# Weight sums moved from VectorE to GpSimd, and all tasks ordered anew, in a threshold attention and gated feed-forward kernel

## The chip, the cores and the metric

The kernel runs on one core of a Trainium2 chip. A core has five engines, each with its own instruction queue that is worked off strictly in order: TensorE (PE, matmuls; its weight loads are shown as PEld), VectorE (DVE), ScalarE (ACT), GpSimd (POOL) and SyncE (SP, which here only issues transfers). Data lies in SBUF, 128 partitions wide; matmuls write to PSUM banks. The metric is the device time of one execution in microseconds; lower is better.

## What is computed

Everything is float32. Attention comes first: batch 8, 8 heads, 576 tokens, head width 64. In each row of scores only the values within `tau` = 0.02 of the row's maximum are kept; a softmax over them weights the values. Its output, laid out as 4608 tokens by 512, goes through a feed-forward layer of width 2048.

```
scores = q @ k^T / 8;  scores = where(scores >= rowmax - tau, scores, -1e9)
attn   = exp(scores - rowmax);  attn = attn / (sum(attn) + 1e-9);  x = attn @ v      # (8,8,576,64) -> (4608,512)
h = x @ w_in;   g = h * sigmoid(1.702 h);   out = g @ w_out
```

## The kernel before

**Attention** works on 32 pairs of heads, numbered n; four pairs make one batch of 576 tokens. For a pair, PE writes scores transposed into PSUM (`scores`, L590), ACT copies them to SBUF (`keep`, L607), DVE reduces them to a row maximum (`in_groups`, L613, and the small steps after it), DVE subtracts the maximum (`sub`, L687), ACT masks and exponentiates (`mask` L694, `exps` L698), and PE multiplies by the values (`values`, L709). Pairs 0 to 3 have their softmax sums made by PE too. `place_x` (DVE, L813) divides by the sums and writes a slice of x into one of six `xT` tiles. From pair 6 on, the `values` of one pair and the `scores_run` of a later one run on PE as one uninterrupted stretch.

**Feed-forward** works on 18 blocks of 256 tokens, in order; one chain of dependencies (`ffn`) strings all its PE work together. Blocks 0 and 1 run the first layer plainly (`mm1_0`, L886, then `tanh` L843 on ACT and `gelu_0` L892 on DVE). The other products are done in Strassen-like form: seven products of quarter matrices (P1, P2, P6, P7, P4, P5, P3) instead of eight, where the quarters of weights and of tokens are first added or subtracted. `product1` (L954) does this for the first layer of one block, `product4` (L1127) for two blocks at once from block 7 to block 12, `product` (L1431) for the second layer. The last 1024 tokens, blocks 14 to 17 (`TAIL`), use the form twice over: each of the seven products is again split into seven (`product2` L1278, `product3` L1387). For that second level the sums of quarters of quarters of the weights are needed: three 128x512 sums for each of seven matrices of each layer, 42 in all.

**These 42 sums** are made by `scrap_sum` (L1197) long before they are used, one instruction per sum, and written to DRAM by SP. Eight of the fourteen triples are made along with blocks 3 to 6 (`EARLY_EXTRAS`, in the function `seven`): the triple's tile is an `xT` tile, and two transfers (`extra_out`, L1201) carry it out. The other six are made along with block pairs 7, 9 and 11 (`LATE_EXTRAS`, in `seven4`), two triples each: every sum goes to the one buffer `scrap`, and the next may begin only when the transfer of the last (`scrap_out`, L1207) is done. In the tail `extra_in` (L1240) and `extra2_in` (L1315) bring them back.

**Weights of the first layer's sums** for `product4` flow back from DRAM through four small buffers: `w_flow` (L1104), a transfer issued from POOL's queue, twelve per pair of blocks. A block pair's first two go out when the previous blocks no longer use the buffers' space, and P6 is the first product that reads them.

**Weight conversion.** The inputs `moe_w_in` and `moe_w_out` come as 64-bit floats and are turned into float32 in 32 pieces of 128x512: SP loads a piece into a staging area (`load_w`, L510), ACT computes one part in two steps (`cv_power` L520, `cv_power2` L524), DVE the other and joins them (`cv_whole` L538, `cv_end` L545). Pieces 0 to 15 are `w_in`, 16 to 31 `w_out`. A staging slot comes free when `cv_end` is done.

**The order.** Each engine's program order is not written by hand. Every step is a `task` with an engine, a planned cost, a rank, what it must follow and which buffers it takes and gives back. `run_in_order` plays all tasks through in planned time: an engine that is free takes, of the tasks that are ready, the one with the lowest rank, and the instructions are emitted in that order. Ranks are the pair's number plus a bias for each function; the tables `EARLY`, `SECOND`, `LATER`, `CV`, `W_RANK` and `L_RANK` hold the biases. Attention on PE goes ahead of feed-forward whenever it is ready. 40 short matmul tasks (`stay_warm`, L1497) are taken only where nothing else is ready in the plan.

Of the kernel before, what the change touches and what calls it, by code (L numbers as in the profile page):

```python
# [32 lines left out]
def kernel(  # L33
# [96 lines left out]
    for x in ("raw0", "raw1", "qkT0", "qkT1", "mb"):  # L130
# [3 lines left out]


    EARLY = {
        "add_row": 15.24,
        "cross_max": 16.53,
        "exps": 169.66,
        "in_groups": 24.3,  # L140
        "keep": 18.51,
        "load_qk": 52.9,
        "load_v": 77.19,
        "mask": 220.69,
        "one_row": 73.01,
        "over_halves": -24.07,
        "over_tiles": 93.0,
        "place_x": 110.06,
        "row_in": 2.01,
        "row_out": -23.95,  # L150
        "scores_run": 0.25,
        "spread_max": -9.31,
        "spread_sums": 55.95,
        "sub": 109.63,
        "sums_by_pe": 219.69,
        "turn_in": 106.44,
        "turn_rows": -16.16,
        "turned": 157.69,
        "values": 15.27,
    }  # L160
    SECOND = {
        "add_row": 48.97,
        "cross_max": -30.15,
        "cross_sums": 46.61,
        "exps": 425.25,
        "in_groups": 788.95,
        "keep": 52.62,
        "load_qk": -8.72,
        "load_v": 50.95,
        "mask": 273.1,  # L170
        "over_halves": 13.47,
        "over_tiles": 10.11,
        "place_x": -14.67,
        "prep": 130.42,
        "row_in": -47.42,
        "row_out": 60.46,
        "scores_run": -14.82,
        "spread_max": -16.4,
        "sub": 29.57,
        "sums_in": 53.13,  # L180
        "sums_out": -17.8,
        "turn_rows": -30.52,
        "turn_sums": 63.82,
        "values": -7.11,
    }
    LATER = {
        "add2": -163.47,
        "add3": -23.7,
        "copy2": 51.25,
        "copy3": 34.37,  # L190
        "cross_max": 60.81,
        "cross_sums": 61.03,
        "exps": 93.29,
        "in_groups": 10.85,
        "keep": 85.17,
        "load_qk": -13.0,
        "load_v": -2.27,
        "mask": 11.12,
        "over_halves": -26.94,
        "over_tiles": -36.69,  # L200
        "place_x": -13.68,
        "prep": 24.88,
        "s_level1": -6.85,
        "s_level2": -6.85,
        "scores_run": 22.76,
        "silu2": 83.51,
        "spread_max": -74.31,
        "sub": -0.09,
        "sums_in": -524.28,
        "sums_out": -75.26,  # L210
        "turn_sums": 83.71,
        "values": -57.82,
    }
    CV = {
        "cv_end": 69.28,
        "cv_power": -47.14,
        "cv_power2": -20.47,
        "cv_whole": -4.05,
        "load_w": 14.98,
    }  # L220

    LAG = {"PE": 0.26, "DVE": 0.18, "ACT": 0.22, "POOL": 0.18, "SP": 0.1}
# [957 lines left out]
    def scrap_sum(second, x, k):  # L1180
        u1 = u2 = scrap
        if x in SOONER[second]:
            if k == 0:
                places["extra", second, x] = x_home()
            u1, u2 = (places["extra", second, x][:, ts(z, BANK)] for z in range(2))
        if second:
            y = right2(x)
            b11, b12, b21, b22 = (y[:, ts(c, 4), ts(n, HT)] for c in range(2) for n in range(2))
            u1, u2 = four(u1), four(u2)
            o, a, b, op = ((u1, b12, b11), (u2, b22, u1), (u1, b21, u2))[k] + (ALU.subtract,)  # L1190
        else:
            y = left1(x)
            a11, a12, a21, a22 = (y[:, c, ts(f, BANK)] for f in range(2) for c in range(2))
            o, a, b, op = (
                (u1, a21, a22, ALU.add), (u2, u1, a11, ALU.subtract), (u1, a12, u2, ALU.subtract)
            )[k]
        nc.vector.tensor_tensor(out=o, in0=a, in1=b, op=op)  # L1197

    def extra_out(second, x, part):
        n, m = ((2, 0), (1, 2))[part]  # L1200
# [329 lines left out]
    FFU = 1.727  # L1530
    T_RANK = FIRST

    W_RANK = (51.17, 144.32, 134.71, 686.68, 50.64, 279.44)
    W_TIME = 1.8
    WARM = 40
    ROUND_BY_ACT = range(0)
# [415 lines left out]
    def seven(blk):  # L1952
        b = -(-(blk + 1) * BLK // S) - 1
        xs = [placed[n] for n in range(NPAIR * (b + 1))]
        xd = []
        if not w_done:
            w_sums()
        a = None
        for second_layer, n in EARLY_EXTRAS.get(blk, ()):
            for k in range(3):  # L1960
                a = task(
                    "DVE", 0.6, FIRST, scrap_sum, second_layer, n, k,
                    after=[w_done[-1], t_ready[-1], ffn[-1], a], take=("xT",) if k == 0 else (),
                )
                if k:
                    a = task("SP", 0.55, FIRST, extra_out, second_layer, n, k - 1, after=[a], take=RING[0])
                    a = transfer("DMS", (3.0, 1.5)[k - 1], a, 2, give=RING[0] + (("xT",) if k == 2 else ()))
            (extra_out_done, extra2_out_done)[second_layer][n] = a
        for x in range(4):
            xd.append(task("DVE", 0.34, FIRST, x_sum, blk, x, after=(xd[-1:] or xs) + last1))  # L1970
        keeps, adds, gs = {}, {}, {}

        def gelued(y, f, h, after):
            gs.setdefault((f, h), {})[y] = task(
                "ACT", 0.5, FIRST, silu1, y, f, h, after=after,
                give=("psM",) if (f, h) == (1, 0) else (),
            )

        for x in (P1, P2, P6, P5, P7, P4, P3):
            for y in range(2):  # L1980
                after = ffn[-1:] + xs
                if x in (P6, P7, P4, P5):
                    after = after + xd[{P6: 1, P7: 2, P4: 3, P5: 0}[x]:][:1]
                if x in (P6, P7, P5, P3):
                    after = after + [w_done[{P6: 1, P7: 2, P5: 0, P3: 3}[x]]]
                if x in (P6, P7, P4):
                    after = after + [keeps[{P6: P1, P7: P6, P4: P7}[x], y]]
                if x == P3:
                    after = after + [adds[P5, 0], adds[P5, 1]]
                ffn.append(task(  # L1990
                    "PE", 1.785, LAST, product1, blk, x, y, after=after,
                    take=("psM",) if x == P1 else ("psA",) if x in (P2, P5) and y == 0 else (),
                    give=("xT",) if x == P3 and y else (),
                ))
                if x in (P1, P6, P7):
                    keeps[x, y] = task("ACT", 0.5, FIRST, keep1, x, y, after=ffn[-1:])
                if x in (P2, P3) and y:
                    for z in range(2):
                        adds[x, z] = task(
                            "DVE", 0.6, FIRST, add1, x, z,  # L2000
                            after=ffn[-1:] + [keeps[{P2: P1, P3: P6}[x], z]],
                            give=("psA",) if z else (),
                        )
                        if x == P3:
                            gelued(z, 0, 1, [adds[P3, z], gs[1, 1][1]])
                if x == P7:
                    adds[P5, y] = task(
                        "DVE", 0.6, FIRST, add1, P5, y, after=[keeps[P7, y], ffn[-2 - y]],
                    )
                if x == P4:  # L2010
                    gelued(y, 1, 0, ffn[-1:])
                    if y:
                        for f, h, z in ((0, 0, P2), (1, 1, P5)):
                            for w in range(2):
                                gelued(w, f, h, [adds[z, w], gs[1, 0][w]])
        last1[:] = ffn[-1:]
        sums = [
            task("DVE", 1.33, FIRST, s_sums, blk, y, after=[gs[x][y] for x in ((0, 0), (0, 1), (1, 1))])
            for y in range(2)
        ]  # L2020
        minus = [task("DVE", 0.6, FIRST, s_minus, blk, y, after=[sums[y]]) for y in range(2)]
        second(blk, {P1: gs[0, 0], P2: gs[1, 0], P4: gs[1, 1]}, sums, minus)
# [8 lines left out]
    def seven4(blk):  # L2031
# [11 lines left out]
        a = None  # L2043
        for second_layer, x in LATE_EXTRAS[blk]:
            for k in range(3):
                a = task("DVE", 0.6, FIRST, scrap_sum, second_layer, x, k, after=freed + [t_ready[-1], a])
                a = task("SP", 0.55, FIRST, scrap_out, second_layer, x, k, after=[a], take=RING[0])
                a = transfer("DMS", 1.4, a, 2, give=RING[0])
            (extra_out_done, extra2_out_done)[second_layer][x] = a
# [270 lines left out]
            next_blk += 1  # L2320

    crossed = {"max": [], "sums": []}
    L_RANK = (6.9, -26.88, 69.44, 31.9, 9.2, 38.16, 10.43, 63.15, 25.98, 364.83, 169.13, -0.14, 11.11, -6.6, 5.42, 34.59, 27.46, 64.99, 61.43, -2.14, 71.89, -4.67, 27.56, 35.73)

    def load_rank(n, which):
        return L_RANK[3 * n + which] if 3 * n < len(L_RANK) else 0.0
# [242 lines left out]
```

## Time and profile before

| | |
|---|---|
| median of 3 runs | 1224.37 us (1223.91 to 1226.27) |
| profiled execution, span from first to last instruction | 1224.7 us |
| PE / PEld busy | 1206.5 us (99%) / 995.8 us (81%) |
| DVE busy | 1077.1 us (88%), 1683 instructions |
| ACT busy | 797.6 us (65%), 1197 instructions |
| POOL busy | 69.3 us (6%), 114 instructions |
| DMA, mean over the span | 111 GB/s, 136.09 MB |

How to read it: the profiled execution is listed with its span alone, which lies 0.3 us above the median of the runs. A row of a group gives the instruction's line, its engine, what it writes and reads, its shape, how often it ran, its total busy time and the mean of one, and how long the engine stood idle just before it. A row of a timeline gives start, duration and the same names, and in brackets the idle time ahead of it with what ended that. PE's busy time counts matmuls whose ends are modelled, so that neighbours overlap by a fraction of a microsecond. Trace counts of float32 matmuls are twice the number in the program's listing.

### The profile page before, as it was taken

To read this page: it belongs to the slowest core of one execution; us is meant where nothing else is said; L and a number is where in the kernel's file an instruction comes from. 1 tells how busy PE (TensorE), PEld (TensorE's weight loads), DVE (VectorE), ACT (ScalarE), POOL (GpSimd) and SP (SyncE) were. 2 spreads that over 40 slices of the span, in tenths; PEclk is the share of its full clock that TensorE was granted. 3 is DMA by queue.
4 is the path that set the end of the run, shared out by engine and by line. 5 is a ranking of instruction groups with operands and counts; after the bars stand their busy time and mean duration, and the time that the engine had idled before them with its cause. 6 is when DMAs were issued, how large, how long until landed. Compare 5 with 4: busy or idle time off the path is not lost.

```text
span 1224.7 us, 26240 instructions
## 1 busy us (share of the span) xinstructions
PE 1206.5 (99%) x10672; PEld 995.8 (81%) x10672; DVE 1077.1 (88%) x1683; ACT 797.6 (65%) x1197; POOL 69.3 (6%) x114
## 2 busy tenths in 40 slices
PE   8999999999999999999999999999999999999998
PEld 5656777797978888888777777787787797999998
DVE  6989998878898998898699977998799989999797
ACT  6999977675765766684686468756875676340340
POOL 0111231100000000000100010001100000000000
PEclk9999999999999999999999999999999999999999
DMA  8957769492323241224423252225322351444443
GB/s 222 249 108 190 173 142 170 103 210 65 93 50 110 49 120 48 75 72 135 101 67 99 66 133 72 59 77 128 92 49 67 87 139 39 139 129 140 140 137 104
DMA packets 201193, 136.09 MB, mean 111 GB/s; under 512 B 146864, under 2 KB 163376, under 8 KB 200944
## 3 DMA queue, kind: packets, MB, share of 16 engines
q1 hardware_dynamic: 189712, 110.21, 34.0%
q0 software_dynamic: 10672, 23.90, 9.4%
q8 instruction: 84, 1.38, 0.5%
q10 hardware_dynamic: 688, 0.30, 0.1%
q14 instruction: 37, 0.30, 0.1%
HBM read 103.28 MB, written 23.75 MB: 104 GB/s over the span
## 4 chain that ended last, share of the span: by engine, by line
PE 88%; ACT 8%; DMA 2%; DVE 1%; issue 1%; SPq 0%; DVEq 0%; ACTq 0%
PE ops L1431 28%; PE pv L709 10%; PE ps L590 10%; PE hps L954 7%; PE hps L1127 7%; PE ps L954 5%; PE ps L1127 5%; PE hps L1278 4%; PE ops L1387 4%; PE ps L1278 3%; PE ps L1387 3%; ACT arena L698 2%; ACT arena L694 2%; PE hps L886 2%; ACT arena L607 2%; DMA arena<-in_moe_w_in_dram 1%
## 5 line engine op out<-in xcount | busy, mean ns | idle before, releaser
L613 DVE TRANSPOSE_TENSOR_REDUCE part<-arena 128x36 f32<-128x1152 f32 x300 | 363.8, 1239 | 52.6 <-ACT arena L607 40.2
L607 ACT COPY arena<-ps 128x576 f32<-128x576 f32 x288 | 171.2, 642 | 95.6 <-PE ps L590 95.5
L694 ACT ACTIVATE arena<-arena 128x1152 f32<-128x1152 f32 (+1 forms) x160 | 164.6, 1064 | 66.6 <-DVE arena L687 66.2
L1431 PE MATMUL ops<-w_out,arena 128*128 128x256 f32 x896 | 203.0, 381 | 0.1
L1431 PEld LDWEIGHTS ops<-w_out,arena 128*128 128x128 f32 x896 | 168.5, 190 | 28.5 <-issue 5.3
L687 DVE TENSOR_TENSOR arena<-arena 128x1152 f32<-128x1152 f32 (+1 forms) x150 | 180.9, 1241 | 0.7
L698 ACT ACTIVATE arena<-arena,shift 128x1152 f32<-128x1152 f32 (+1 forms) x160 | 179.7, 1156 | 1.4
L590 PE MATMUL ps<-arena 64*64 64x288 f32 x2304 | 172.1, 408 | 8.0 <-ACT arena L607 6.1
L709 PE MATMUL pv<-arena 64*64 64x288 f32 x2176 | 159.2, 405 | 0.0
L590 PEld LDWEIGHTS ps<-arena 64*64 64x64 f32 x2304 | 81.9, 132 | 71.5 <-ACT arena L607 29.7
L1431 PE MATMUL ops<-arena 128*128 128x256 f32 x576 | 129.1, 379 | 0.0
L709 PEld LDWEIGHTS pv<-arena 64*64 64x64 f32 x2176 | 80.3, 133 | 53.0 <-issue 9.0
L1431 PEld LDWEIGHTS ops<-arena 128*128 128x128 f32 x576 | 109.2, 190 | 15.8 <-issue 0.9
L1292 ACT COPY arena<-hps 128x512 f32<-128x512 f32 x44 | 25.7, 584 | 59.5 <-PE hps L1278 59.5
L632 ACT ACTIVATE other<-red,minus_gap 32x18 f32<-32x18 f32 x118 | 36.2, 307 | 35.1 <-DVE red L622 33.6
L1104 POOL DMA_DIRECT2D arena<-wrow x36 | 19.5, 540 | 619.0 <-DVE arena L1197 321.8
L886 PE MATMUL hps<-xT,w_in 128*128 128x256 f32 x232 | 51.2, 381 | 0.9 <-DVE arena L892 0.9
L886 PEld LDWEIGHTS hps<-xT,w_in 128*128 128x128 f32 x232 | 43.6, 190 | 8.6 <-DVE arena L892 1.5
L1453 DVE SCALAR_TENSOR_TENSOR osb<-ops,osb 128x256 f32<-128x256 f32 x98 | 39.2, 411 | 11.5 <-PE ops L1431 10.5
L954 PEld LDWEIGHTS hps<-xT,w_in 128*128 128x128 f32 x384 | 44.2, 192 | 1.5 <-issue 0.9
L954 PE MATMUL hps<-xT,w_in 128*128 128x128 f32 x384 | 45.3, 276 | 0.0
L1127 PE MATMUL hps<-xT,w_in 128*128 128x256 f32 x192 | 43.4, 379 | 0.0
(228 smaller groups left out, 1859.9 us busy)
## 6 DMA issues: line engine op xcount, KB each, us to landing
arena<-in_v_dram SPq DMA_DIRECT2D x128, 144.0 KB
arena<-exu SPq DMA_DIRECT2D x42, 256.0 KB
arena<-ext SPq DMA_DIRECT2D x39, 256.0 KB
arena<-wrow POOLq DMA_DIRECT2D x36, 256.0 KB, 3.3
arena<-in_k_dram SPq DMA_DIRECT2D x112, 72.0 KB
arena<-in_q_dram SPq DMA_DIRECT2D x112, 72.0 KB
out_dram<-osb SPq DMA_DIRECT2D x28, 256.0 KB
arena<-row_s SPq DMA_DIRECT2D x48, 144.0 KB
```

What stands on the lines that cost most here:

```text
L590: nc.tensor.matmul(ps[ts(c, KT), h, 0:SH], lhsT=mats[n, 1][ts(h, D), ts(j, KT)], rhs=mats[n, 0][ts(h, D), ts(c, SH)], start=True, stop=True,)
L607: nc.scalar.copy(out=sT[n, t][:, u], in_=pss.pop((n, j))[:, :, 0:SH])
L613: nc.vector.tensor_reduce(out=stats[n, op][:, t * 2 * QB : min(2 * t + 2, NK) * QB], in_=sT[n, t].rearrange("p u h (g d) -> p (u h g) d", ...
L687: engine.tensor_tensor(out=s, in0=s, in1=mbs[n].unsqueeze(1).to_broadcast(list(s.shape)), op=ALU.add if n in BY_DMA else ALU.subtract,)
L694: nc.scalar.activation(out=s, in_=s, func=AF.Prelu, alpha=STEEP)
L698: nc.scalar.activation(out=s, in_=s, func=AF.Exp, scale=SCALE, bias=shift)
L709: nc.tensor.matmul(o[c][ts(h, D), 0:SH], lhsT=left(j, h)[ts(c, KT)], rhs=sT[n, t][ts(c, KT), u, h, :], start=(j == 0), stop=(j == NK - 1),)
L886: nc.tensor.matmul(hidden[j][:, ts(i, BLK)], lhsT=w_in[:, c, ts(j, P)], rhs=xTs[i][:, c, :], start=(c == 0), stop=(c == NDC - 1), skip_gro ...
L954: nc.tensor.matmul(o[:, ts(j, HT)], lhsT=left[:, c, ts(4 * y + j, P)], rhs=right[:, c, :], start=(x in (P1, P2, P5) and j + c == 0), stop= ...
L1127: nc.tensor.matmul(o[:, ts(j, BLK)], lhsT=left[:, c, ts(j, P)], rhs=right[:, c, :], start=(x in (P1, P2, P5) and j + c == 0), stop=(j + c ...
L1278: nc.tensor.matmul(o[:, ts(j, HT)], lhsT=left[:, ts(j, P)], rhs=right, start=(m in (P1, P2, P5) and j == 0), stop=(j == 3), skip_group_che ...
L1431: nc.tensor.matmul(banks[blk][k][:, ts(o, HM)], lhsT=left[:, j, :], rhs=right[:, j, :], start=(j == 0), stop=(j == HF - 1),)
```

## The change

`scrap_sum` issues its instruction on GpSimd, and the two places that make its tasks book it on POOL with a planned cost of 1.3 us, where it was DVE with 0.6 us. All six tables of ranks have new values. Nothing else differs: the same instructions, transfers, buffers and dependencies; on which engine 42 of them stand, and the order on every engine, are new.

```diff
@@ scrap_sum
-        nc.vector.tensor_tensor(out=o, in0=a, in1=b, op=op)
+        nc.gpsimd.tensor_tensor(out=o, in0=a, in1=b, op=op)
@@ seven: EARLY_EXTRAS
-                    "DVE", 0.6, FIRST, scrap_sum, second_layer, n, k,
+                    "POOL", 1.3, FIRST, scrap_sum, second_layer, n, k,
@@ seven4: LATE_EXTRAS
-                a = task("DVE", 0.6, FIRST, scrap_sum, second_layer, x, k, after=freed + [t_ready[-1], a])
+                a = task("POOL", 1.3, FIRST, scrap_sum, second_layer, x, k, after=freed + [t_ready[-1], a])
@@ tables of ranks, all entries; some of them
     EARLY = {
...
-        "exps": 169.66,
+        "exps": 218.659396,
...
     LATER = {
-        "add2": -163.47,
+        "add2": 218.879808,
...
-    W_RANK = (51.17, 144.32, 134.71, 686.68, 50.64, 279.44)
+    W_RANK = (48.948553, 218.656324, 220.911367, 648.238789, 209.699298, 477.491922)
...
-    L_RANK = (6.9, -26.88, 69.44, 31.9, 9.2, 38.16, 10.43, ...
+    L_RANK = (-88.352359, -377.791989, 203.787298, 98.253766, 49.342752, -419.169055, -251.720956, ...
```

More of the change, by code (lines that the diff above doesn't have):

```diff
@@ L136 @@
     EARLY = {
-        "add_row": 15.24,
-        "cross_max": 16.53,
-        "exps": 169.66,
[L140 to L159, printed above, removed]
+        "add_row": -26.779956,
+        "cross_max": -186.11076,
+        "exps": 218.659396,
+        "in_groups": -921.329572,
+        "keep": -376.476703,
+        "load_qk": 28.45392,
+        "load_v": 55.937037,
+        "mask": 258.382077,
+        "one_row": 754.390311,
+        "over_halves": -177.607232,
+        "over_tiles": -242.559764,
+        "place_x": 353.472828,
@@ L160 @@
+        "row_in": -524.546255,
+        "row_out": -204.477791,
+        "scores_run": 73.864427,
+        "spread_max": -665.338509,
+        "spread_sums": -255.466111,
+        "sub": 276.088418,
+        "sums_by_pe": 395.294969,
+        "turn_in": 1536.802593,
+        "turn_rows": -980.064642,
+        "turned": 86.363115,
+        "values": -93.163536,
     }
     SECOND = {
[L162 to L184, printed above, removed]
+        "add_row": 276.088418,
@@ new lines @@
+        "cross_max": -240.949838,
+        "cross_sums": -329.737322,
+        "exps": 504.025884,
+        "in_groups": 987.755038,
+        "keep": 46.111798,
+        "load_qk": -533.474947,
+        "load_v": 332.525097,
+        "mask": 481.823863,
+        "over_halves": -194.246828,
+        "over_tiles": 543.631566,
+        "place_x": 800.597733,
+        "prep": 454.948868,
+        "row_in": -31.868144,
+        "row_out": 80.112526,
+        "scores_run": -23.727141,
+        "spread_max": 634.529675,
@@ L185 @@
+        "sub": 806.709122,
+        "sums_in": 528.330009,
+        "sums_out": 403.59979,
+        "turn_rows": -550.558759,
+        "turn_sums": -21.685664,
+        "values": 818.914814,
     }
     LATER = {
-        "add2": -163.47,
[L188 to L212, printed above, removed]
+        "add2": 218.879808,
+        "add3": -4.036609,
+        "copy2": -530.184332,
@@ new lines @@
+        "copy3": 209.512485,
+        "cross_max": 1588.737584,
+        "cross_sums": 546.442989,
+        "exps": 614.129479,
+        "in_groups": 183.39928,
+        "keep": 353.976442,
+        "load_qk": 354.397262,
+        "load_v": 796.965227,
+        "mask": 4.965175,
+        "over_halves": 55.173625,
+        "over_tiles": 792.89621,
+        "place_x": -14.016573,
+        "prep": 1023.214781,
+        "s_level1": 1308.273433,
+        "s_level2": 381.073959,
+        "scores_run": -30.208042,
@@ L213 @@
+        "silu2": 49.468221,
+        "spread_max": 417.352117,
+        "sub": 46.78672,
+        "sums_in": -951.376181,
+        "sums_out": 718.483673,
+        "turn_sums": 144.651892,
+        "values": -771.795118,
     }
     CV = {
[L215 to L219, printed above, removed]
+        "cv_end": 5.647379,
+        "cv_power": -62.099737,
+        "cv_power2": -63.051811,
+        "cv_whole": 224.118761,
@@ L220 @@
+        "load_w": 41.452962,
     }
@@ L2322 @@
     crossed = {"max": [], "sums": []}
-    L_RANK = (6.9, -26.88, 69.44, 31.9, 9.2, 38.16, 10.43, 63.15, 25.98, 364.83, 169.13, -0.14, 11.11, -6.6, 5.42, 34.59, 27.46, 64.99, 61.43, -2.14, 71.89, -4.67, 27.56, 35.73)
+    L_RANK = (-88.352359, -377.791989, 203.787298, 98.253766, 49.342752, -419.169055, -251.720956, 316.979634, 531.734811, 464.681494, 298.790272, -81.491014, 99.216053, 450.74533, 707.475464, 354.348049, -186.433338, -612.234764, 270.826085, -446.603159, 423.489084, 582.149219, 643.218533, -435.166825)
     def load_rank(n, which):
```

## The prediction

> **What bounds the kernel now.** I read the page first (busy times, clock, chain), then stretches of time, then the engines' timelines where PE is not full.
>
> ```profile
> span 1224.7 us, 26240 instructions
> ...
> PE 1206.5 (99%) x10672; PEld 995.8 (81%) x10672; DVE 1077.1 (88%) x1683; ACT 797.6 (65%) x1197; POOL 69.3 (6%) x114
> ...
> PE 88%; ACT 8%; DMA 2%; DVE 1%; issue 1%; SPq 0%; DVEq 0%; ACTq 0%
> ```
>
> The chain that ended last is PE for 88% of the span, ACT for 8%. Where the 8% lies, the next view tells: it gives, for a stretch, its length and the busy time of PE, PEld, DVE, ACT, POOL, then granted clock, DMA share, GB/s.
>
> ```profile
> 0.00:150.00 150.00, 135.29 (x1667) 90.96 (x1668) 128.68 (x202) 137.24 (x202) 27.79 (x51) 0.99 0.76 187
> 150.00:1200.00 1050.00, 1049.70 (x8816) 883.55 (x8815) 931.03 (x1435) 659.48 (x993) 41.52 (x63) 1.00 0.40 101
> 1200.00:1225.00 25.00, 21.50 (x193) 21.31 (x191) 17.41 (x48) 0.83 (x3) 0.00 (x0) 1.00 0.31 96
> ```
>
> From 150 to 1200 us PE stands idle for 0.30 us in all, at full clock. DVE, which the change relieves, has 931 of 1050 us there and PE never waits for it long enough to show. So the time is: when PE's unbroken stretch begins, plus a fixed amount of PE work, plus the end. Only the first 150 us and new stalls can move it.
>
> The head, on PE:
>
> ```profile
> 108.39 1.99 PE L886 MATMUL hps<-xT,w_in 128*128 128x256 f32 x8
> 111.27 26.17 PE L886 MATMUL hps<-xT,w_in 128*128 128x256 f32 x120 [0.89 <-DVE arena L892]
> ...
> 146.21 1.25 PE L590 MATMUL ps<-arena 64*64 64x288 f32 x16 [1.52 <-ACT arena L607]
> ...
> 176.00 1.44 PE L1497 MATMUL up<-eye,ones 64*64 64x128 f32 x12
> 177.51 7.17 PE L1431 MATMUL ops<-w_out,arena 128*128 128x256 f32 x32
> ```
>
> Feed-forward starts at 108.39, waits 0.89 us for the first `gelu_0`, then runs; 1.52 us are lost at 146 behind ACT's `keep`; at 176 PE fills 1.44 us with warm-up matmuls. And on ACT, up to the first `tanh` (L843):
>
> ```profile
> 16.42 0.77 ACT L520 ACTIVATE w_in<-w_out,rebias 128x512 f32<-128x512 int16 x1 [0.80 <-DMA w_out<-in_moe_w_in_dram]
> ...
> 28.17 0.75 ACT L520 ACTIVATE w_in<-arena,rebias 128x512 f32<-128x512 int16 x1 [2.43 <-DMA arena<-in_moe_w_in_dram]
> ...
> 144.25 0.77 ACT L520 ACTIVATE w_out<-arena,rebias 128x512 f32<-128x512 int16 x1 [1.55 <-DMA arena<-in_moe_w_out_dram]
> ```
> ```profile
> 8.00:30.00 22.00, 17.88 (x33) 1.00 0.93 235
> 30.00:111.00 81.00, 79.96 (x111) 0.98 0.73 180
> ```
>
> The second fence is ACT alone: idle 4.1 us from 8 to 30, 1.0 us from 30 to 111. ACT sets when feed-forward starts; its three waits are all for weight pieces.
>
> **The change, part by part.**
>
> *PE's work.* Compared in the two program orders, PE issues the same matmuls of every shape, and changes between 64-row and 128-row matmuls 75 times in both. Cost 0. Attention runs further ahead in the new order, by up to one pair near the end; PE is full in either case, so 0.
>
> *42 sums leave DVE.* The rows are L1197's alone (length, DVE busy, count):
>
> ```profile
> 290.00:540.00 250.00, 16.16 (x24) 1.00 0.29 77
> 540.00:575.00 35.00, 4.03 (x6) 1.00 0.39 106
> 640.00:700.00 60.00, 4.03 (x6) 1.00 0.26 74
> 770.00:830.00 60.00, 4.04 (x6) 1.00 0.23 64
> ```
>
> DVE is freed of 28.3 us, 0.67 us each, all of it where PE doesn't wait. Worth 0; with that cover (PE's own work) gone it would be worth at most 28.3.
>
> *42 sums come to POOL.* No row shows a two-input GpSimd operation. The nearest:
>
> ```profile
> L1475 POOL TENSOR_SCALAR_AFFINE_SELECT eye<-eye 128x128 f32<-128x128 f32 x1 | 0.3, 287 | 0.1
> ...
> L1467 POOL MEMSET rebias<- 128x1 f32 x1 | 0.1, 98 | 0.0
> ```
>
> 287 ns for 128 columns less 98 ns for one is 1.48 ns a column: 0.86 us for 512 columns with one input, 1.61 us if a second input is read after the first. I take 1.2 us, between them, since the second input costs something; both ends stay. POOL gets 50 us of work (36 to 68) over 550 us, hidden while what stands behind it is on time. The Trainium skill (GPSIMD Engine Reference, section 3.1) gives 4497 ns for a two-input add of 2048 columns; a quarter of that, an estimate, is 1.1 us, which would change no term here.
>
> *What stands behind the sums on POOL.* The early 24 stand behind the last row transfers and in front of nothing but the late ones; they hold their `xT` tile some 1.6 us longer per triple (3 times 1.2 less 0.67), which `place_x` would notice only if all six tiles were out: 0. The first late six stand in front of all twelve `w_flow` of blocks 7 and 8, and each but the first waits for the transfer of the one before, so the chain is:
>
> ```profile
> 540.99 0.68 DVE L1197 TENSOR_TENSOR arena<-w_in 128x512 f32<-128x512 f32 x1
> ...
> 572.68 0.65 DVE L1197 TENSOR_TENSOR arena<-arena,arena 128x512 f32<-128x512 f32 x1
> ```
> ```profile
> 567.96 0.35 SPq L1207 DMA_DIRECT2D exu<-arena  x1
> ```
> ```profile
> 568.21 0.62 POOL L1104 DMA_DIRECT2D arena<-wrow  x1 [321.75 <-DVE arena L1197]
> 569.95 0.57 POOL L1104 DMA_DIRECT2D arena<-wrow  x1 [1.11 <-DMA exu<-arena]
> ```
> ```profile
> arena<-wrow POOLq DMA_DIRECT2D x36, 256.0 KB, 3.3
> ```
> ```profile
> 580.00 3.45 PE hps L1127 x16
> ```
>
> P6 of block 7 starts at 580.00 and reads the first piece, which lands 3.3 us after an issue of 0.6 us: it must be issued by 576.1. The first sum may run at 541.0. A step is 1.2 us of sum plus the transfer, 2.0 us (567.96 to 569.95), plus handing on, some 0.3 us: 3.5 us; the sixth sum ends at 541.0 + 5 x 3.5 + 1.2 = 559.7. At the pace they had on DVE, (572.68 - 540.99) / 5 = 6.3 us, it ends at 573.7, still 2.4 us early. Cost 0; from 6.8 us a step on, each further microsecond of pace costs PE 5. The other two sets of six have about 60 us of second-layer work to hide in. The transfers stay on SP's queue; their place among its loads changes, which I can't price beyond that pace.
>
> *Start of feed-forward.* In the new ACT order the first `tanh` comes behind two more L520 and one more L524 (16 and 15 against 14 and 14; 54 `keep` in both). Steps on the chain:
>
> ```profile
> 42.16 1.61 ACT arena L607 x3
> ...
> 85.45 0.67 ACT w_in L520
> ...
> 115.84 1.22 ACT w_out L524 x2
> ```
>
> 2 x 0.67 + 0.61 = 1.95 us more. Against it: SP loads three pieces in a row early, moving a pair of k loads behind, and ACT has 1.7 us more `keep` and `turned` work ahead of the piece it waited 2.43 us for. So that wait should go. What is late next is the moved k load:
>
> ```profile
> 30.00:40.00 10.00, 9.01 (x138) 8.10 (x140) 9.88 (x18) 9.82 (x15) 2.05 (x4) 0.83 1.03 316
> ```
> ```profile
> 31.29 1.78 PE L568 MATMUL ps<-eye,arena 64*64 64x64 f32 x33 [0.38 <-DMA arena<-in_k_dram]
> ...
> 36.50 1.41 DVE L578 COPY arena<-ps 128x576 f32<-128x576 f32 x2
> ```
>
> It now comes after a weight piece and a v load, 512 + 4 x 144 KB, 1.1 MB, at 316 GB/s 3.5 us. Its transposes ended at 33.1 and DVE copied them at 36.5, 3.4 us to spare: its scores come when they did, and ACT has meanwhile done two `keep` more, 1.1 us. That much is recovered, I take it, and the rest of the 2.43 is not. Bounds: nothing, or 3.5 of the 5.1 us idle. So +0.9 us, from -1.5 to +2.0.
>
> *The loss at 146.* The new order issues six `w_out` pieces earlier on SP, before the next pair's loads, and converts up to four of them sooner; the transfer ACT waited for until 144.25 should be there. But ACT also reaches this place 1 to 2 us later. Between 0 and -1.5, I take -1.1.
>
> *The warm-up at 176.* It covers the last `tanh` and `gelu_0`, without which the second layer can't start; the new order has no warm-up left there, so PE will simply be idle as long. 0.
>
> *The end.* The last ten groups of matmuls and SP's last three transfers are the same in both orders. 0.
>
> *New stalls in 1070 us of reordered work* can't be gains, since 0.30 us is all there is. I take +0.3 (a few sub-microsecond waits), up to 5.
>
> Sum against the profiled execution: 1224.7 + 0.9 - 1.1 + 0.3 = 1224.8; at the level of the runs, whose median is 0.3 us below that span, **1224.5 us**. That is no change: 0.2% (2.4 us) is about what a measurement of this kernel can tell.
>
> **The rivals.**
>
> *Faster: ACT catches up.* If its waits at 16 and 28 go and no later load replaces them, feed-forward starts 1.5 us sooner in spite of the added conversions, and the 1.5 at 146 goes too: 1224.4 - 3.0 = 1221.4. All of ACT's 5.1 idle less 1.95, plus 1.52 and 0.89 on PE, bounds it: 5.5 us, 1218.9. For it speaks that the waits are for weights and the weights are loaded earlier; against it that DMA is at its limit there.
>
> *Slower: the head gets worse.* The k load eats all that is won: +2.0. And PE comes to the scores behind which it lost 1.52 us after 60 matmuls where it had 64, 1.7 us sooner (8 of the trace's, 26.17 / 120 each), while ACT comes later, so that loss grows by 1.0 instead of going: 1224.4 + 3.0 = 1227.4.
>
> *Slower: GpSimd holds DVE.* In 540 to 573 DVE is nearly full:
>
> ```profile
> 540.00:573.00 33.00, 33.00 (x256) 26.20 (x255) 32.37 (x48) 20.90 (x31) 1.73 (x3) 1.00 0.36 98
> ```
>
> Five sums less leave 29.0 us (32.37 - 5 x 0.67). If every one of six GpSimd sums keeps a DVE instruction waiting for its 1.2 us, it is 36.2: 3.2 us too much, and PE's second layer waits for its sums: 1224.4 + 3.2 = 1227.6. It decides from (33.0 - 29.0) / 6 = 0.67 us held per sum. The Trainium skill (SBUF — State Buffer, Who interferes with whom) states that a DVE instruction with two SBUF inputs and a GpSimd instruction that reads SBUF share a read interface and the later one blocks entirely. No trace here shows it yet; by that rule one-input work such as L613 goes free, so the rival's full price is an upper one.
>
> *Slower: `w_flow` comes late.* Pace 7.8 us, as when SP's queue holds the transfers back: 5 us, 1229.4.
>
> **How the numbers follow.** No change 0.44 (1222.5 to 1226.5 by itself), faster 0.22, worse head 0.14, held DVE 0.12, late `w_flow` 0.08. So faster 0.22, same 0.44, slower 0.34. The range runs from 1220, past the faster case's own figure towards its bound, to 1231, past the late `w_flow`; about 0.15 is left out.
>
> **What would show it.** Right: PE again idle under 1 us from 150 to 1200; the first unbroken L886 row near 112; no wait at 146; ACT's wait at 28 gone; L1197 on POOL at 0.9 to 1.6 us; the first L1104 near 568, released by PE. Wrong: an L1127 row waiting for a DMA, L687 or L1054 longer than before while L1197 runs, any PE wait of more than 1 us after 180, or a start of L886 before 110.

## The result: 0.8% slower

The changed kernel took 1233.94 us (median of four runs, 1231.72 to 1238.16) against 1224.14 us: a ratio of 1.0081 (95% interval 1.006 to 1.0102), 9.8 us more. It was run once more beside three experiments: 1233.41 us, ratio 1.0084 (1.0071 to 1.0097). The forecast was 1224.5 us, in a range of 1220 to 1231.

The page of the profiled execution of the changed kernel, first its busy times, then the chain that ended last:

```profile
span 1232.9 us, 26299 instructions
...
PE 1206.7 (98%) x10672; PEld 997.9 (81%) x10672; DVE 1063.6 (86%) x1641; ACT 795.9 (65%) x1195; POOL 127.3 (10%) x156
...
PE 74%; DVE 11%; ACT 9%; DMA 3%; issue 2%; POOL 0%; DVEq 0%; ACTq 0%; POOLq 0%
```

PE's work is what it was (1206.5 us before). DVE gave up 42 sums of 0.67 us, 28.3 us of rows, but is only 13.5 us less busy (1077.1 to 1063.6). Not all 28.3 could show, since neighbouring DVE rows overlap a little: with the sums left out (the third experiment) it is 22.0 us less busy (1055.1). The other 8.5 have come back. And it now stands on the chain with 11%, where it had 1%. The same three stretches as before the change (length, then PE, PEld, DVE, ACT, POOL):

```profile
0.00:150.00 150.00, 136.70 (x1688) 94.39 (x1689) 132.97 (x206) 140.27 (x206) 27.76 (x51) 1.00 0.76 194
150.00:1200.00 1050.00, 1040.25 (x8722) 874.01 (x8721) 904.88 (x1371) 653.98 (x984) 99.57 (x105) 1.00 0.38 98
1200.00:1233.00 33.00, 29.78 (x266) 29.55 (x264) 25.70 (x67) 1.66 (x6) 0.00 (x0) 0.99 0.35 110
```

In the head PE is idle 13.3 us (14.7 before); at the end 3.1 (3.2). But between 150 and 1200, where it had been idle for 0.30 us, it is now idle for 9.75. PE's timeline says where (the bracket is the idle time before the row and who ended it):

```profile
110.81 24.71 PE L886 MATMUL hps<-xT,w_in 128*128 128x256 f32 x112 [2.35 <-DVE arena L892]
...
178.63 3.72 PE L1431 MATMUL ops<-w_out,arena 128*128 128x256 f32 x16 [1.23 <-DVE arena L892]
183.68 3.69 PE L1431 MATMUL ops<-arena 128*128 128x256 f32 x16 [1.33 <-ACT osb L1446]
...
569.41 1.26 PE L590 MATMUL ps<-arena 64*64 64x288 f32 x16 [1.15 <-ACT arena L607]
...
673.13 0.71 PE L590 MATMUL ps<-arena 64*64 64x288 f32 x8 [1.44 <-ACT arena L607]
...
808.15 0.71 PE L590 MATMUL ps<-arena 64*64 64x288 f32 x8 [1.34 <-ACT arena L607]
...
1113.97 1.16 PE L1387 MATMUL ops<-arena,arena 128*128 128x128 f32 x8 [0.37 <-ACT osb L1393]
...
1116.84 1.16 PE L1387 MATMUL ops<-arena 128*128 128x128 f32 x8 [0.64 <-DVE arena L1343]
```

So the 8.2 us between the two spans (1224.7 and 1232.9) come from three places:

- 150 to 250 us: 4.78 us idle (100 - 95.22), 0.20 before, of which 2.56 at 178 and 183; the 1.44 us of warm-up matmuls that stood at 176 have gone into the head, so they come off: 3.1 us;
- 569, 673 and 808 us: 3.93 us, each beside late sums;
- 1114 us: 1.01 us.

The rest, head and end, is within half a microsecond of nothing. That is so for these two executions. In every later run of this record a run's time is 1.7 to 2.1 us longer than its core's span, and 1.8 in the changed kernel's profiled one (1234.72 against 1232.9). So the profiled execution of the kernel before took, by this estimate, some 1226.5 us: 2 us above the median, not at its level. Its head is the longest of the five profiled kernels with the old ranks: PE is idle 14.71 us before 150, where the other four have 12.26 to 14.14. That fits the medians lying 9.8 us apart and the spans only 8.2.

The three late places share one picture; this is the one at 673. DVE, POOL and ACT of the changed kernel, one timeline each:

```profile
654.89 0.69 DVE L1040 TENSOR_TENSOR arena<-arena 128x512 f32<-128x512 f32 x1
655.50 1.76 DVE L1037 TENSOR_TENSOR arena<-arena 128x512 f32<-128x512 f32 x1
657.29 0.69 DVE L1040 TENSOR_TENSOR arena<-arena 128x512 f32<-128x512 f32 x1
...
659.10 1.77 DVE L1110 TENSOR_TENSOR arena<-xT 128x512 f32<-128x512 f32 x1
...
671.58 0.39 DVE L622 TENSOR_REDUCE red<-part 128x18 f32<-128x162 f32 x1
```
```profile
654.89 1.82 POOL L1197 TENSOR_TENSOR arena<-w_in,arena 128x512 f32<-128x512 f32 x1 [2.18 <-DMA ext<-arena]
658.86 1.46 POOL L1197 TENSOR_TENSOR arena<-w_out 128x512 f32<-128x512 f32 x1 [2.15 <-DMA ext<-arena]
```
```profile
672.00 0.42 ACT L764 COPY other<-red 32x18 f32<-32x18 f32 x2 [1.97 <-DVE red L622]
672.44 1.18 ACT L607 COPY arena<-ps 128x576 f32<-128x576 f32 x2
```

L1037 and L1110 do 128x512 sums that take 0.68 us; the two that meet a GpSimd sum take 1.76 and 1.77, 1.08 more, and end some 0.55 us behind it (the sum ends at 656.71, L1037 at 657.26): they do their work when it is done. They count as busy, not idle: a held instruction shows only as a long one. The GpSimd sum too is long when it meets DVE (1.82; 1.27 by itself). DVE works without a gap from there to L622, which ends 2.2 us later than it would; ACT waits 1.97 us for it in L764 (`cross_sums`), with the `keep` (L607) queued behind it that PE needs. That is a reading; the runs below test it.

I worked the holds out over the whole trace: each DVE instruction that overlaps a sum, against the median of the same operation and shape beside none. In the changed kernel 12 are held, 10.1 us in all. Every held one has two inputs in SBUF (L687, L1110, L1040, L1045, L1037, and L769 of only 18 columns, 1.26 us in place of 0.14). Of 26 overlapping L613 (one input) and some 25 with an input in PSUM (L973, L1173, L1453, L813) none is 0.1 us longer. The Trainium skill (SBUF — State Buffer, Who interferes with whom) has this as a rule, and that a GpSimd instruction which only writes does not hold; the trace agrees, and the third experiment shows the last part.

### The profile page after: what moved, and what is told of

Its sections match the earlier page's. It is cut to its first block, busy times and chain, and to the rows that moved or that the text cites. A ratio compares the mean times of both kernels' runs of the same rounds, so it can differ in the third digit from the quotient of the medians.

```text
span 1232.9 us, 26299 instructions
## 1 busy us (share of the span) xinstructions
PE 1206.7 (98%) x10672; PEld 997.9 (81%) x10672; DVE 1063.6 (86%) x1641; ACT 795.9 (65%) x1195; POOL 127.3 (10%) x156
## 4 chain that ended last, share of the span: by engine, by line
PE 74%; DVE 11%; ACT 9%; DMA 3%; issue 2%; POOL 0%; DVEq 0%; ACTq 0%; POOLq 0%
PE ops L1431 21%; PE pv L709 8%; PE ps L590 8%; PE hps L1127 7%; PE hps L954 6%; PE ps L1127 5%; PE ps L954 5%; PE hps L1278 4%; PE ops L1387 3%; DVE part L613 3%; PE ps L1278 3%; PE ps L1387 2%; ACT arena L607 2%; ACT arena L694 2%; DVE arena L687 1%
## 5 line engine op out<-in xcount | busy, mean ns | idle before, releaser
L613 DVE TRANSPOSE_TENSOR_REDUCE part<-arena 128x36 f32<-128x1152 f32 x300 | 365.8, 1240 | 61.8 <-ACT arena L607 52.3
L607 ACT COPY arena<-ps 128x576 f32<-128x576 f32 x288 | 171.2, 643 | 102.3 <-PE ps L590 99.5
L687 DVE TENSOR_TENSOR arena<-arena 128x1152 f32<-128x1152 f32 (+1 forms) x150 | 183.7, 1260 | 2.3 <-DMA arena<-row 1.4
L590 PE MATMUL ps<-arena 64*64 64x288 f32 x2304 | 172.6, 408 | 12.2 <-ACT arena L607 8.2
L709 PE MATMUL pv<-arena 64*64 64x288 f32 x2176 | 159.2, 405 | 0.2 <-ACT arena L607 0.2
L590 PEld LDWEIGHTS ps<-arena 64*64 64x64 f32 x2304 | 83.0, 132 | 74.2 <-ACT arena L607 29.5
L709 PEld LDWEIGHTS pv<-arena 64*64 64x64 f32 x2176 | 80.5, 133 | 52.0 <-issue 7.3
L886 PE MATMUL hps<-xT,w_in 128*128 128x256 f32 x232 | 51.7, 382 | 2.4 <-DVE arena L892 2.4
L886 PEld LDWEIGHTS hps<-xT,w_in 128*128 128x128 f32 x232 | 43.6, 190 | 10.6 <-DVE arena L892 3.2
L1453 DVE SCALAR_TENSOR_TENSOR osb<-ops,osb 128x256 f32<-128x256 f32 x98 | 39.0, 409 | 9.6 <-PE ops L1431 6.4
L1127 PE MATMUL hps<-xT,w_in 128*128 128x256 f32 x192 | 43.6, 380 | 0.0
```

Source lines behind the costliest of these rows:

```text
L590: nc.tensor.matmul(ps[ts(c, KT), h, 0:SH], lhsT=mats[n, 1][ts(h, D), ts(j, KT)], rhs=mats[n, 0][ts(h, D), ts(c, SH)], start=True, stop=True,)
L607: nc.scalar.copy(out=sT[n, t][:, u], in_=pss.pop((n, j))[:, :, 0:SH])
L613: nc.vector.tensor_reduce(out=stats[n, op][:, t * 2 * QB : min(2 * t + 2, NK) * QB], in_=sT[n, t].rearrange("p u h (g d) -> p (u h g) d", ...
L687: engine.tensor_tensor(out=s, in0=s, in1=mbs[n].unsqueeze(1).to_broadcast(list(s.shape)), op=ALU.add if n in BY_DMA else ALU.subtract,)
L709: nc.tensor.matmul(o[c][ts(h, D), 0:SH], lhsT=left(j, h)[ts(c, KT)], rhs=sT[n, t][ts(c, KT), u, h, :], start=(j == 0), stop=(j == NK - 1),)
L886: nc.tensor.matmul(hidden[j][:, ts(i, BLK)], lhsT=w_in[:, c, ts(j, P)], rhs=xTs[i][:, c, :], start=(c == 0), stop=(c == NDC - 1), skip_gro ...
```

## The experiments

All times are medians; the ratio is to the kernel before, run beside them on the same chip.

**1 to 4: the engine, the order, the reading, the ranks.** Kernel before, only the engine:

```diff
-        nc.vector.tensor_tensor(out=o, in0=a, in1=b, op=op)
+        nc.gpsimd.tensor_tensor(out=o, in0=a, in1=b, op=op)
```

> The order of before, with nothing changed but the engine of the 42 sums (GpSimd). Two theories of the 9.8 us lost. HELD: a GpSimd sum makes a VectorE instruction with two inputs beside it wait (L1037 took 1.76 us where it takes 0.68), and this causes the three PE waits at 569, 673 and 808 us, 3.9 us in all. ORDER: all 9.8 us come from the new order of the tasks, and the sums' engine costs nothing. HELD expects PE waits near the late sums here too (540 to 570, 650 to 700, 770 to 815), 1 to 4 us in all: 1225 to 1228. ORDER expects 1224.1, within 0.5 us.

Measured: 1226.45 us, ratio 1.0013 (1.0004 to 1.0021): 1.6 us slower. The number fits HELD, the place doesn't. PE's timeline in this kernel has its waits beside early sums, none beside late ones:

```profile
327.50 3.84 PE L954 MATMUL hps<-arena,w_in 128*128 128x128 f32 x32 [0.71 <-ACT arena L968]
...
395.70 3.84 PE L954 MATMUL hps<-arena,w_in 128*128 128x128 f32 x32 [0.42 <-ACT arena L968]
...
464.62 3.84 PE L954 MATMUL hps<-arena,w_in 128*128 128x128 f32 x32 [0.73 <-ACT arena L968]
```

Just ahead of the first, four L687 meet three sums. DVE and POOL of this kernel, then DVE of the kernel before at the same work:

```profile
317.31 7.80 DVE L687 TENSOR_TENSOR arena<-arena 128x1152 f32<-128x1152 f32 x4
```
```profile
318.27 1.53 POOL L1197 TENSOR_TENSOR xT<-arena,xT 128x512 f32<-128x512 f32 x1 [8.94 <-DMA ext<-xT]
319.76 2.38 POOL L1197 TENSOR_TENSOR xT<-arena 128x512 f32<-128x512 f32 x1
322.23 2.27 POOL L1197 TENSOR_TENSOR xT<-xT,arena 128x512 f32<-128x512 f32 x1
```
```profile
321.13 4.55 DVE L687 TENSOR_TENSOR arena<-arena 128x1152 f32<-128x1152 f32 x4
```

The two engines take turns: 3.25 us more for four instructions. In all, this kernel's holds are 19.9 us, against the 28.3 us of rows that left DVE.

Kernel after, the engine alone taken back (bookings and order stay new):

```diff
-        nc.gpsimd.tensor_tensor(out=o, in0=a, in1=b, op=op)
+        nc.vector.tensor_tensor(out=o, in0=a, in1=b, op=op)
```

> The order of the changed kernel, with the 42 sums put back on VectorE at the same places in the order. ORDER expects the whole loss: 1232 to 1238, with the PE waits at 176 to 250 us (3.3 us) and 1114 us (1.0 us) as they were. HELD expects those too, since no sum runs there, but says that at 569, 673 and 808 us a wait of 1.1 us per held instruction is exchanged for 0.67 us of work per sum, so 1231 to 1236. Below 1230 the sums' engine would be the larger part of the loss.

Measured: 1232.82 us, ratio 1.0069 (1.0054 to 1.0085). With no GpSimd sum at all most of the loss is there, the late waits too:

```profile
564.69 1.26 PE L590 MATMUL ps<-arena 64*64 64x288 f32 x16 [1.13 <-ACT arena L607]
...
668.80 0.72 PE L590 MATMUL ps<-arena 64*64 64x288 f32 x8 [1.34 <-ACT arena L607]
...
804.08 0.71 PE L590 MATMUL ps<-arena 64*64 64x288 f32 x8 [1.57 <-ACT arena L607]
```

So holding is not needed for them: 0.67 us of DVE's own per sum does the same. That what PE feels is DVE's lateness, from whatever cause, is the reading that the next experiment tests. Kernel after, without the sums' reads:

```diff
-        nc.gpsimd.tensor_tensor(out=o, in0=a, in1=b, op=op)
+        nc.gpsimd.memset(o, 1.0)
```

> The changed kernel in its own order; each of the 42 sums is replaced by GpSimd filling the same 512 columns with ones, so that GpSimd reads nothing (the sums are left out, and what is computed from them is not the reference's). HELD expects L1037, L1040 and L1110 at 0.68 us again and the PE waits at 569, 673 and 808 us gone or under 0.4 us each: 3.9 us less than the changed kernel, 1230. ORDER expects the waits to stay: 1233 to 1235.

Measured: 1227.0 us, ratio 1.0018 (1.0009 to 1.0027), 6.9 us below the changed kernel, where HELD expected 3.9. (The profiled execution, 1230.63 us, was the longest of the twelve.) Not one DVE instruction beside a fill is 0.1 us longer than elsewhere, and PE's stretches (length, PE busy) show the late waits gone, 0.04 us of 350:

```profile
150.00:250.00 100.00, 96.32 (x707) 1.00 0.67 131
...
500.00:850.00 350.00, 349.96 (x2803) 1.00 0.35 91
850.00:1200.00 350.00, 348.99 (x2927) 1.00 0.37 105
```

With the sums costing DVE nothing, neither as work nor as holds, the new order is 2 us slower than the old; with them 8 to 10. The idle time before 250 and near 1114 stays, so that part belongs to the order. Last, the ranks of before with the new bookings (and the sums on GpSimd):

```diff
-                    "DVE", 0.6, FIRST, scrap_sum, second_layer, n, k,
+                    "POOL", 1.3, FIRST, scrap_sum, second_layer, n, k,
...
-                a = task("DVE", 0.6, FIRST, scrap_sum, second_layer, x, k, after=freed + [t_ready[-1], a])
+                a = task("POOL", 1.3, FIRST, scrap_sum, second_layer, x, k, after=freed + [t_ready[-1], a])
```

> The ranks of before, with the sums on GpSimd and booked there, so that the planner makes a new order from the old ranks (PE's list of instructions differs in 549 lines). ORDER, in its strict form (the ranks are at fault), expects 1223 to 1226. If any new order loses because the old ranks were tuned to the old bookings, 1226 to 1236. HELD adds 1 to 4 us to either.

Measured: 1259.62 us, ratio 1.0282 (1.0267 to 1.0298), some 20 us above all that I had allowed. The old ranks did not survive the new bookings: PE stands idle for 16.7 us between 1050 and 1100. PE in that stretch (length, PE busy, count, granted clock), its longest wait, and DVE:

```profile
1050.00:1100.00 50.00, 33.29 (x269) 0.80 0.25 81
```
```profile
1086.77 2.05 PE L1278 MATMUL hps<-arena 128*128 128x128 f32 x8 [8.92 <-DVE arena L1250]
```
```profile
1083.62 0.95 DVE L813 TENSOR_TENSOR xT<-pv,arena 128x64 f32<-128x64 f32 x4 [5.88 <-DMA arena<-row_s]
```

The new plan leaves a row transfer (`sums_in`) too little time ahead of the `place_x` (L813) that waits for it. Idle time is not all of the loss: PE is also busy for 10.4 us longer than before (1216.9 us against 1206.5). In this stretch the granted clock is 0.80, and the eight matmuls behind the wait take 2.05 us where eight of the same line take 1.06 at 1093. So the old ranks could not be kept with these bookings; the ranks of the changed kernel do 26 us better than this and still 10 worse than the kernel before.

**5 to 8: where in the new order.** The changed kernel once more, for its scatter:

> The changed kernel once more, beside the next three on the same chip, since the four runs of it lie 6.4 us apart. Expected 1232 to 1236, with PE waits at 569, 673 and 808 us again.

Measured: 1233.41 us (1232.41 to 1237.53), waits of 1.16, 1.45 and 1.44 us at 567, 671 and 806. But the waits at 178 and 183 us are not in this execution, whose span is 1230.6. Only the late sums left out:

```diff
-        nc.gpsimd.tensor_tensor(out=o, in0=a, in1=b, op=op)
+        nc.gpsimd.tensor_tensor(out=o, in0=a, in1=b, op=op) if x in SOONER[second] else nc.gpsimd.memset(o, 1.0)
```

> The changed kernel; only the 18 late sums are left out (GpSimd fills their columns with ones), the 24 early ones run on GpSimd. What is computed from the late sums is not the reference's. LATE theory: the loss that filling all 42 removed came from the late sums, whose held VectorE instructions delay the sums of pairs 17, 20 and 24 (L622), on which ScalarE waits in L764 with L607 queued behind it: expects the PE waits at 569, 673 and 808 us gone, 4 us less than the changed kernel run beside it, and a time within 1 us of the kernel with all 42 filled (2.3 us above before). EARLY theory: the early sums cost the rest (6.9 - 3.9 = 3.0 us): expects 3 us above the all-filled kernel, 5.3 above before.

Measured: 1227.53 us, ratio 1.0032 (1.0019 to 1.0045), 5.9 us below the changed kernel beside it (4 expected), PE again idle for 0.04 us from 500 to 850. LATE is right: the 18 late sums carry nearly all. Whether the early 24 cost something in this order the intervals (1.0032 against 1.0018 in another session) do not settle. Next, ScalarE's order alone, in the list of tasks before they are issued:

```diff
+        for n in (17, 20, 24):
+            x = at("cross_sums", n)
...
+            plan[x : y + 1] = early + [plan[x]] + [i for i in some if i not in early]
```

(`early` is the next two `keep` and PE's tasks up to them.)

> The changed kernel, all sums on GpSimd; on ScalarE alone three pairs of L764 (cross_sums of pairs 17, 20, 24) are moved behind the next two L607. Everything computed, same lists on all other engines. If the waits at 569, 673, 808 us are ScalarE standing in L764 for a late VectorE (held or not), PE no longer waits there: 3.5 to 4 us less than the changed kernel. If VectorE's lateness itself is what PE needs next, the waits come back a few us later at L1431 or L709 and the time stays within 1 us.

Measured: 1232.38 us, ratio 1.0061 (1.0049 to 1.0073): 1 us less by the medians, 2.8 by the ratios, whose intervals just overlap. The three waits are gone, and others come 9 to 26 us behind the places. PE:

```profile
585.87 1.99 PE L1127 MATMUL hps<-xT,w_in 128*128 128x256 f32 x8 [0.60 <-DVE osb L1453]
...
681.88 10.63 PE L1431 MATMUL ops<-w_out,arena 128*128 128x256 f32 x48 [0.64 <-DVE osb L1453]
698.44 1.26 PE L590 MATMUL ps<-arena 64*64 64x288 f32 x16 [0.92 <-ACT arena L607]
...
832.93 1.26 PE L590 MATMUL ps<-arena 64*64 64x288 f32 x16 [0.73 <-ACT arena L607]
```

2.9 us in place of 3.9 to 4.05: ACT's queue decided mostly where DVE's lateness was paid, and only in small part whether. And the same kind of move at 174 us (`behind(x, y)` moves task x to the place just behind task y):

```diff
+        for t in (4, 3, 1):
+            behind(at("mask", 6, t), at("tanh", 15))
+        for k in range(2):
+            behind(at("t_minus", 3, k), at("read", 0, 0) + k)
```

> The changed kernel; on ScalarE alone the last tanh (L843) is moved ahead of three L694 and the first eviction of the second layer (L1446) ahead of two L1013. The PE waits of 1.23 us at 178 and 1.33 us at 183 should shrink by about 1.2 and 1.3 us if ScalarE's order is their cause: 2 to 2.6 us less than the changed kernel. If they are covers of something that is late anyway (gelu_0 on VectorE, a transfer), below 0.7 us less.

Measured: 1235.13 us, ratio 1.0086 (1.0073 to 1.0099): nothing gained. The profiled execution was one where those waits would hardly have been, so it does not settle ScalarE's part in them; and it pays 1.61 us at 201 us for a transfer that adds weights to L1013's result, which the move made later. What goes with the waits is seen by laying the profiles side by side: in the three executions of the new order where ACT waits for the last `w_out` piece at 170 us (3.81, 2.76 and 2.98 us: the changed kernel, the filled one and the one in halves, below), PE is idle 3.7 to 4.8 us between 150 and 250; where the piece is there, 1.9 to 2.1 (this kernel apart, with its new wait). The row of the changed kernel, ACT:

```profile
170.80 0.80 ACT L520 ACTIVATE w_out<-arena,rebias 128x512 f32<-128x512 int16 x1 [3.81 <-DMA arena<-in_moe_w_out_dram]
```

Why the piece is late in some executions stays open; loading it sooner was not tried.

**9 to 11: the engine again, part by part.** In the order of before, only the late or only the early sums on GpSimd:

```diff
-        nc.vector.tensor_tensor(out=o, in0=a, in1=b, op=op)
+        (nc.vector if x in SOONER[second] else nc.gpsimd).tensor_tensor(out=o, in0=a, in1=b, op=op)
```

(early: `not in`.)

> The order of before; only the 18 late sums run on GpSimd, the 24 early ones stay on VectorE. In the order of before with all 42 on GpSimd PE stood idle 0.08 us from 500 to 850 us, so the holds there are hidden: expected 1224.5, within 0.7 us of before, PE idle under 0.5 us from 150 to 1200. If the late sums also cost time in this order: 1226 or more.

Measured: 1224.41 us, ratio 1.0 (0.9991 to 1.0009). The late sums hold ten DVE instructions by 8.7 us in all, and PE is idle for 0.11 us from 500 to 850: the old order hides all that the new one shows.

> The order of before; only the 24 early sums run on GpSimd, the 18 late ones stay on VectorE. If the 1.6 us that all 42 cost in this order are the three PE waits at 327, 396 and 465 us (0.71, 0.42, 0.73), where four L687 took 7.80 us instead of 4.55 beside three sums, they are all here: 1226.0 to 1226.8. If instead the loss is spread over both kinds: 1225.

Measured: 1228.39 us, ratio 1.0026 (1.0017 to 1.0035), more than expected and, by the medians, 2 us more than all 42 together (1.0013; the intervals just overlap). The profile has two of the three waits (0.72 at 331, 0.71 at 467), 1.4 us. The place is confirmed, the size is not. What sets the two kernels apart is not beside the sums: of the 2.4 us between their profiled spans (1226.9 and 1224.5), 1.9 are idle time of PE before 150 us (14.14 and 12.26) and 1.0 longer matmuls (PE busy 1207.8 and 1206.8), while between 150 and 1200 this kernel is idle 0.5 us less. Why heads differ so stays open. Last, the changed kernel with each sum in two halves of 256 columns (`halves` stands for the two slices):

```diff
-        nc.gpsimd.tensor_tensor(out=o, in0=a, in1=b, op=op)
+        [nc.gpsimd.tensor_tensor(out=o[z], in0=a[z], in1=b[z], op=op) for z in halves]
```

> The changed kernel; each of the 42 sums is issued as two GpSimd instructions of 256 columns. If a VectorE instruction is held until the GpSimd instruction that runs has ended, the longest L1037, L1040 and L1110 fall from 1.77 to about 1.3 us (0.68 and half of 1.27), and the PE waits at 569, 673 and 808 us shrink from 4.0 to 2 or 3 us: 1 to 2 us less than the changed kernel (1231.5 to 1232.5). If the engines share by element, or VectorE is held by both halves one after the other, the longest stay at 1.7 and the time at 1233.5.

Measured: 1233.22 us, ratio 1.0069 (1.0055 to 1.0082). The groups of L1110 (minimum/median/maximum in ns), first of the changed kernel, then with halves, and the halves' own:

```profile
L1110 DVE TENSOR_TENSOR arena<-xT x3: 679/679/1766, 552.4 to 794.3; 128x512 f32<-128x512 f32 x3
```
```profile
L1110 DVE TENSOR_TENSOR arena<-xT x3: 679/683/1226, 553.7 to 795.4; 128x512 f32<-128x512 f32 x3
...
L1197 POOL TENSOR_TENSOR xT<-arena,xT x10: 726/730/734, 322.3 to 536.4; 128x256 f32<-128x256 f32 x10
```

The longest fall from 1.77 to 1.23: an instruction is held until the GpSimd instruction that runs has ended, as expected. But more of them are caught, all holds together are 8.9 us in place of 10.1, the three waits still add up to 3.6 us, and the time is the changed kernel's within the intervals.

## Why the prediction was wrong, step by step

The two choices side by side, in ratios to the kernel before:

| | sums on VectorE | sums on GpSimd | sums filled, not read |
|---|---|---|---|
| old order | 1 | 1.0013 | not run |
| new order | 1.0069 | 1.0081, 1.0084 | 1.0018 |

- **PE's work, the end:** right.
- **42 sums off DVE, worth 0:** right in the old order only, from whose rows it was read: with the late sums moved there, nothing changes at all. In the new order DVE's time is worth something: between the sums on DVE and the sums filled lie 5.8 us (1232.82 and 1227.0).
- **The level of the sum:** 1224.7 is a span and 1224.4 a median of times, which are some 1.8 us longer than spans. So the execution that was read lay some 2 us above the median, by this estimate, and not 0.3. The forecast, no change, doesn't hang on it.
- **A sum of 1.2 us on GpSimd** (0.86 to 1.61): 1.27 measured. The Trainium skill's 4497 ns for 2048 columns (GPSIMD Engine Reference, section 3.1) agrees: 512 columns take 1.275 and 256 take 0.730 us, 2.13 ns a column and 0.18 to start, which drawn out to 2048 columns is 4.5 us, an estimate.
- **The `w_flow` chain, cost 0:** right, for another reason than mine. It ends at 580.64 + 2.07, not at 559.7: the first sum runs only at 551.24 and the sixth waits 12.00 us for a transfer queued on SP. But the new order moved P6 of block 7 from 580 to 592.68 as well, and no L1127 waits for a piece. POOL of the changed kernel:

```profile
551.24 1.28 POOL L1197 TENSOR_TENSOR arena<-w_in 128x512 f32<-128x512 f32 x1 [15.18 <-PE ps L954]
...
580.64 2.07 POOL L1197 TENSOR_TENSOR arena<-arena,arena 128x512 f32<-128x512 f32 x1 [12.00 <-DMA exu<-arena]
```

- **The head, +0.9 and -1.1:** right in its signs. The long L886 row begins at 110.81, 0.46 us sooner than in the profiled execution before, but at 111.5 on average of the eight profiled kernels with the new ranks, against 109.4 of the five with the old. ACT's waits at 16 and 28 are gone (idle 1.2 us from 8 to 30 in place of 4.1), and so is PE's wait at 146. The head as a whole came out 0.3 us later in one execution and 0.6 in the other (idle time, with the 1.44 us of warm-up now in it and, in the other, 1.15 us of longer matmuls).
- **The warm-up at 176, 0:** wrong both ways: 2.6 us idle in one execution in place of 1.44, none in the other.
- **New stalls, "+0.3 (a few sub-microsecond waits), up to 5":** this is the step that failed. They are 9.45 us in the profiled execution and 6.84 in the other; 1.44 of each stands where the warm-up stood, so they cost 8.0 and 5.4. About 4 of these are the three waits beside the late sums, 1.0 is at 1114, the rest lies between 150 and 250. I had no row of the new order, took a friendly value because PE had been full in the old one, and gave the bound itself no weight in the forecast. Two of the signs that I had named for being wrong came: PE waits of over 1 us after 180, and L687 longer beside L1197.
- **The rival "GpSimd holds DVE" (0.12, 3.2 us):** its mechanism is what happens, and 4 us of PE's waits lie where the late sums run. But its test failed: it was to decide from 0.67 us held per sum. In the old order the late sums hold DVE by 8.7 us over 18, 0.48 each, and cost nothing; in the new order by 7.7 over 18, 0.43 each, and they cost 4 to 6 us. The threshold came from DVE's room in the old order (33.0 less 29.0 us). The new order leaves less: even 0.67 us of DVE's own work per sum (the second experiment) is too much.

What the new order asks of DVE there is seen by what stands behind `cross_sums` (L764). In the kernel before, at the first late sums, PE has a block's first layer ahead of it, which needs nothing of ACT for the next microseconds. PE and ACT of the kernel before:

```profile
572.93 3.62 PE L1127 MATMUL hps<-xT,w_in 128*128 128x256 f32 x16
576.38 3.62 PE L1127 MATMUL ps<-xT,w_in 128*128 128x256 f32 x16
```
```profile
577.38 0.42 ACT L764 COPY other<-red 32x18 f32<-32x18 f32 x2 [0.21 <-DVE red L622]
```

In the changed kernel PE is in the values and scores of two pairs at that moment (L590 and L709 in turns of 1 us) and needs a `keep` for each turn. Shown is that the late sums' time on DVE, as work or as holds, causes these waits (1232.82 us with them on DVE, 1227.0 with all filled, 1227.53 with the late ones filled). A fill takes GpSimd 0.52 us where a sum takes 1.27, so filling makes GpSimd quicker as well; that this is not what removes the waits rests on the second experiment, which has them with no sum on GpSimd at all. That their place between two pairs is what makes them dear is a reading of the rows. What in the order makes the idle time before 250 us and at 1114 was not found. Whether another order with GpSimd sums could match the old one is open. None of the kernels run beats the one before.

## What to carry to other kernels

Work moved from VectorE to GpSimd does not leave VectorE free when both read two SBUF operands: of the 28.3 us of sums moved here, 10.1 to 19.9 us came back as longer VectorE instructions. Look at the maximum of a group, not its mean: the holds are busy time and no wait shows them. And price a newly sought order as a risk of its own: 0.3 us of idle time in the old one says nothing about the new, and slack measured in one order doesn't carry to another.

## What was not expected of the hardware

A hold catches short instructions as fully as long ones: L769, two inputs of 18 columns, took 1.26 us beside a sum in place of 0.14, while a 128x512 sum on DVE took 1.76 in place of 0.68. And the head scatters: with the same ranks, the long L886 row began at 108.1 to 111.3 us in the profiled executions of five kernels with the old ranks and at 109.3 to 113.2 in eight with the new, more than any term that I had worked out for it.
